# The first whole score tile of a step ahead of the halved tile's first half, and the hold between the two halves on TensorE itself

## The chip, the cores and the metric

The kernel runs on 1 core of one Trainium2 chip. The metric is the device time of one execution in microseconds (us), median of the runs shown.

## What is computed

One transformer-like block on 2048 tokens of width 512, all in float32. With `xn` the layer-normed input:

```python
xn = _layernorm(x, axis=-1)
s = _A_ref(xn, A_wqkv, A_wo)                            # attention, 32 heads of width 16
g = _silu(_B_ref(xn, B_w1, B_b1, B_w2, B_b2))           # gelu MLP, 512 -> 1376 -> 512
return x + s * g
```

The attention is the plain one: scores `q k^T / 4`, softmax over the 2048 keys, times `v`, heads concatenated, times `wo`.

## The kernel before

**Precision and stages.** Operands are split into a high and a low part and multiplied in three terms. A first stage (up to about 480 us of the span) does the layer norm, the projections and the MLP, and already a part of the score tiles described below. The second stage, on which the change bears, is the attention proper: 512 steps and a last one (`for n in range(L + 1)`, line 967). The last 20 steps also do the output projection.

**Units and steps.** The work is cut into 32 units, `u` = one group of 4 heads by one chunk of 512 queries. Each unit takes 16 steps, one for each block of 128 keys. A step does, for its unit and key block:

- **T**, four times (`t_one`, line 733): a transposed score matmul, 128 keys by 512 queries, into a bank of PSUM (L740), and its exponential on ScalarE into SBUF (L742). The row maximum of the scores stands in the matmul as two more rows of the contraction (50 rows = 48 + 2), so it must be known before.
- **V** (`pv_step`, line 799): the four heads' value matmuls of the step before (L805), 32 columns each.

**The score tiles for the maximum.** The maxima come from a second pass over the same scores, 128 queries by 512 keys, that runs ahead: a matmul (`s_mm`, L183) and a maximum on VectorE (`s_max`, L189), in two halves of 256 keys. A job is two such tiles, for head `a` = 0 and `a` = 1 of a pair. Head 0 uses contraction rows from 0 up, head 1 rows from 64 up, so that two matmuls can run side by side in the array; T0 and T1 use the rows from 64 up, T2 and T3 those from 0 up.

A step of the main kind (`want` = 3, steps 2 to 491) does three score tiles. Its order on every engine's queue is a string, written out by hand: `ORDER[3]`, line 40, read by the loop at line 971 and `s_op` (line 209):

- `T`, `V`: as above.
- `S`: a whole tile of 512 keys (`s_whole`, line 198). The first S of a step takes a new job from `jobs` and does head 0, the second does its head 1.
- `X` and `Y`: a cut tile, 256 keys of both heads of another job, in one bank. X (lines 217 to 224) does head 0 into the left half of the bank. Y (lines 226 to 233) does head 1 into the right half, then one maximum over both. The other 256 keys come with the X and Y of the next step.

X and Y write one bank from different rows of the array, so Y must not start before X is done. In the kernel before, a `nop` on GpSimd waits for X (lines 221 and 222), and Y waits for that `nop` (line 228).

**The banks.** The score tiles take turns in three PSUM banks, `s_ring` (line 90; a third one is added at line 774). S takes the first bank of the ring and puts it at the end; X takes one and holds it until Y, which puts it back (line 230). A tile's matmul waits for VectorE's maximum of the tile that had the bank before. T has four banks, one of them used by every fourth T, so T waits for ScalarE's exponential of the T four before.

**Bookkeeping that rides along.** When the last maximum of a unit is issued, `s_end0` (line 239) queues a small maximum on VectorE, puts off two small operations on GpSimd (lines 251 and 252) to the next X (`run_off`, line 224) and has SyncE load the queries of the unit after next. Each V counts four ticks; eight ticks later (`later`, `flush`) a transpose on TensorE (L268) and a copy send the maxima to DRAM. At the end of a unit ScalarE copies the value sums out of PSUM (L812). The schedule is fixed when the program is built; the engines wait for each other by semaphores only.

Of the kernel before, what the change touches and what calls it, by code (L numbers as in the profile page):

```python
# [36 lines left out]
FILL0 = 30  # L37
HB = 4
W2B = 2
ORDER = {0: "TTTTV", 3: "TXSTTSTYV"}  # L40
HC = CH // 2
PAIRED = 28
KB = 3
# [5 lines left out]
def fused(ctx: ExitStack, tc: tile.TileContext, x, wqk, wv, wo, w1, b1, w2, b2, out):  # L49
    nc = tc.nc  # L50
# [35 lines left out]
    SYNC = mybir.DependencyInfo(mybir.DependencyClass.Sync, mybir.DependencyReason.DATA)  # L86
# [5 lines left out]
    def s_tile(held=False):  # L92
        pool = s_ring.pop(0)
        if not held:
            s_ring.append(pool)
        return pool.tile([P, CH], F32, name="ps"), pool
# [58 lines left out]
    done = {u: 0 for u in range(NU)}  # L155
# [16 lines left out]
    def at_of(job):  # L172
        u, st, p = job
        return divmod(st, NCH) if u % (NCH * KB) else divmod(st, NCH)[::-1]

    def s_mm(ps, job, a, c0, k0, w):
        u, st, p = job
        qi, ki = at_of(job)
        if u not in MX:
            MX[u] = qring.tile([P, GH, NCH, NCH, 2], F32, name="mx")  # L180
        r = slice(64 * a, 64 * a + 3 * DH)
        k0 += ki * CH
        return nc.tensor.matmul(ps[:, c0:c0 + w], QS[u][r, p, qi * P:(qi + 1) * P],  # L183
                                kts[u // NCH % KB][p][r, k0:k0 + w], start=True, stop=True).ins

    def s_max(ps, job, heads, parts):
        u, p = job[0], job[2]
        qi, ki = at_of(job)
        nc.vector.tensor_reduce(MX[u][:, 2 * p:2 * p + 2, qi, ki][:, heads, parts], ps.rearrange("p (n c) -> p n c", c=HC), axis=AX.X, op=OP.max)  # L189
        done[u] += 1  # L190
        if ended:
            s_end0(ended.pop())
        if done[u] == 64:
            ended.append(u)
        if done[NU - 1] == 64:
            s_end0(ended.pop())

    def s_whole(job, a):
        ps = s_tile()[0]
        s_mm(ps, job, a, 0, 0, CH)  # L200
        s_max(ps, job, a, slice(0, 2))
# [5 lines left out]
    jobs, whole, cut, put_off = [], [], [], []  # L207

    def s_op(op):
        if op == "S":  # L210
            if whole:
                s_whole(whole.pop(), 1)
            else:
                whole.append(jobs.pop(0))
                s_whole(whole[0], 0)
        elif op == "X":
            if not cut:
                cut[:] = [jobs.pop(0), 0]
            ps, pool = s_tile(True)
            x = s_mm(ps, cut[0], 0, 0, cut[1] * HC, HC)  # L220
            token = nc.gpsimd.nop().ins
            tc.add_manual_dep(token, x.name, SYNC, reason="row tile done")
            cut[2:] = [ps, pool, token]
            run_off()
        else:
            job, n, ps, pool, token = cut
            y = s_mm(ps, job, 1, HC, n * HC, HC)
            tc.add_manual_dep(y, token.name, SYNC, reason="other row tile")
            s_max(ps, job, slice(0, 2), n)
            s_ring.append(pool)  # L230
            cut[1] += 1
            if n:
                cut.clear()

    def run_off():
        while put_off:
            put_off.pop(0)()
# [76 lines left out]
    for j in range(len(pairs)):  # L314
        for h in range(2):
# [9 lines left out]
            n = 2 if nd < len(parts) and parts[nd][2] and ready - nd > room else 1  # L325
            n = max(n, need - 2 * (left - 1))
# [233 lines left out]
    s_when, put, row = [], [0], [0, 0]  # L560
# [387 lines left out]
    for t in range(NW):  # L948
        n = DONE + 2 * t
# [6 lines left out]
    for i, t in enumerate(late):  # L956
        n = L - 2 * len(late) - 1 + 2 * i
# [9 lines left out]
    for n in range(L + 1):  # L967
        ua, ka = divmod(n, 16)
        want = due(n) - due(n - 1)
        i = 0  # L970
        for op in ORDER[want] if n > 1 else ("TTTTV", "TTSTSVT")[n]:
            if op in "SXY":
                s_op(op)
            elif op == "V":
                if n:
                    pv_step(*divmod(n - 1, 16))
                for _ in range(4):
                    tick()
                flush()
            else:  # L980
                if EARLY <= 4 * n + i < 4 * L:
                    t_one(ua, ka, i % 2, 1 - i // 2)
                for f, args in todo.get((n, i), []):
                    f(*args)
                i += 1
# [54 lines left out]
```

## Time and profile before

| | us |
|---|---|
| median of 3 runs | 1596.07 (1595.79 to 1596.75) |
| span of the profiled execution | 1594.7 |
| TensorE matmuls busy | 1587.6 (100%) |
| TensorE weight loads busy | 913.2 (57%) |
| VectorE busy | 1382.8 (87%) |
| ScalarE busy | 1260.1 (79%) |
| GpSimd busy | 373.0 (23%) |

The span is the time of the profiled execution from its first to its last instruction; what lies around it belongs to the run. PE is TensorE's matmuls, PEld its weight loads (each matmul's load has a row of its own), DVE VectorE, ACT ScalarE, POOL GpSimd, SP SyncE; a q behind the name is the engine's sequencer. A row of the timeline has the start in us from the span's start, the time that the row covers, the engine, line, operation, tiles (out<-in) and how many instructions are merged in it; in brackets stands the idle time of the engine before it and who ended it. Matmuls are pipelined: their starts overlap the ones before, and a busy PE is not yet a PE at its peak.

### The profile page before, as it was taken

The page shows a single profiled execution, that of the slowest core. Times are in us where ns is not written, and L with a number is a line of the kernel's source. Part 1 is how long each engine was busy: PE and PEld are TensorE (multiplying, and loading weights), DVE is VectorE, ACT ScalarE, POOL GpSimd, SP SyncE. Part 2 cuts the span into 40 slices and gives each one's busy share as a digit, 9 for nine tenths or more (in the row PEclk, how much of TensorE's full clock was granted, in tenths as well). Part 3 has the DMA queues.
Part 4 walks back from the last instruction along what each step waited for, and adds up shares of the span by engine and source line. Part 5 has one row for each costly group of instructions (what it writes and reads, how often), then busy time and mean ns, then how long its engine had stood idle before and what let it go on. Part 6 is the DMA issues. An engine that isn't in the chain of part 4 may idle for free.

```text
span 1594.7 us, 32234 instructions
## 1 busy us (share of the span) xinstructions
PE 1587.6 (100%) x12144; PEld 913.2 (57%) x12144; DVE 1382.8 (87%) x2261; ACT 1260.1 (79%) x2520; POOL 373.0 (23%) x394
## 2 busy tenths in 40 slices
PE   9999999999999999999999999999999999999998
PEld 8899999999884444444444444444444444444445
DVE  7598898989888999999999989999999999999735
ACT  4324333434349999999999999999999999999984
POOL 4145575756650001000100200100010000000142
PEclk9999999999999999999999999999999999999999
DMA  6626343454431113111410411311131111110252
GB/s 205 150 59 164 106 135 107 158 140 123 126 93 54 32 35 66 29 39 44 82 30 21 71 40 30 61 39 29 31 70 30 31 29 36 36 29 22 59 192 100
DMA packets 74651, 116.89 MB, mean 73 GB/s; under 512 B 23012, under 2 KB 24292, under 8 KB 73320
## 3 DMA queue, kind: packets, MB, share of 16 engines
q1 hardware_dynamic: 70748, 101.89, 22.8%
q0 software_dynamic: 3264, 12.35, 3.9%
q8 instruction: 96, 1.57, 0.4%
q14 instruction: 59, 0.48, 0.1%
q10 hardware_dynamic: 484, 0.60, 0.1%
HBM read 84.35 MB, written 25.97 MB: 69 GB/s over the span
## 4 chain that ended last, share of the span: by engine, by line
PE 98%; DVE 1%; DMA 1%; POOL 0%; issue 0%; ACT 0%; SPq 0%; DVEq 0%; POOLq 0%
PE pv L805 32%; PE ps L183 18%; PE pst L740 16%; PE ps L591 12%; PE pst L591 7%; PE ps L740 5%; PE ps L80 3%; PE pv L591 2%; PE ps L459 1%; PE pst L80 1%; DMA raw<-in_wqk 0%; DVE st L418 0%; PE pst L441 0%; DMA xt<-in_x 0%; PE pst L459 0%
## 5 line engine op out<-in xcount | busy, mean ns | idle before, releaser
L189 DVE TENSOR_REDUCE mx<-ps 128x2 f32<-128x512 f32 x2048 | 1299.5, 685 | 149.4 <-PE ps L183 68.8
L742 ACT ACTIVATE slot<-pst 128x512 f32<-128x512 f32 x1533 | 831.0, 612 | 21.6 <-PE pst L740 12.7
L805 PE MATMUL pv<-slot,vsb 128*32 128x512 f32 x4096 | 545.3, 605 | 0.0
L183 PE MATMUL ps<-kt,slot 48*128 48x512 f32 (+1 forms) x1364 | 393.5, 376 | 0.0
L740 PE MATMUL pst<-qt,kt 50*128 50x512 f32 x1149 | 372.7, 432 | 0.6 <-DVE gt L673 0.4
L740 PEld LDWEIGHTS pst<-qt,kt 50*128 50x128 f32 x1149 | 178.6, 184 | 279.9 <-ACT slot L742 264.3
L742 ACT ACTIVATE slot<-ps 128x512 f32<-128x512 f32 x515 | 315.5, 613 | 3.7 <-PE ps L740 0.5
L183 PEld LDWEIGHTS ps<-kt,slot 48*128 48x128 f32 x1364 | 210.6, 184 | 34.8 <-DVE mx L189 21.6
L591 PE MATMUL ps<-slot,w1h 64*128 64x512 f32 x1088 | 218.0, 393 | 0.2 <-ACT junk L605 0.2
L183 PE MATMUL ps<-kt,qz 48*128 48x512 f32 x512 | 212.4, 415 | 0.0
L183 PE MATMUL ps<-slot,slot 48*128 48x512 f32 (+1 forms) x598 | 172.8, 376 | 0.0
L740 PE MATMUL ps<-qt,kt 50*128 50x512 f32 x387 | 160.3, 416 | 0.0
L591 PEld LDWEIGHTS ps<-slot,w1h 64*128 64x128 f32 x1088 | 151.4, 185 | 8.3 <-ACT junk L605 2.7
L805 PEld LDWEIGHTS pv<-slot,vsb 128*32 128x32 f32 x4096 | 80.6, 108 | 120.2 <-issue 112.2
L591 PE MATMUL ps<-slot,w1l 64*128 64x512 f32 x544 | 141.7, 393 | 0.0
L378 POOL TENSOR_TENSOR hl<-hg,hh 128x512 fp32r<-128x512 f32 x76 | 96.7, 1295 | 129.6 <-ACT hh L377 82.5
L605 ACT ACTIVATE junk<-ident_r 1x1 f32<-1x1 f32 x92 | 18.0, 196 | 120.8 <-PE pst L591 113.6
L740 PE MATMUL pst<-qt,slot 50*128 50x512 f32 x384 | 112.5, 415 | 0.0
L251 POOL CAST nmh<-nm 128x16 fp32r<-128x16 f32 x32 | 6.3, 197 | 413.7 <-PE pst L740 184.7
L183 PEld LDWEIGHTS ps<-kt,qz 48*128 48x128 f32 x512 | 93.7, 183 | 16.3
L183 PEld LDWEIGHTS ps<-slot,slot 48*128 48x128 f32 x598 | 92.5, 184 | 15.7 <-DVE mx L189 10.9
L740 PEld LDWEIGHTS ps<-qt,kt 50*128 50x128 f32 x387 | 71.1, 184 | 44.0 <-ACT slot L742 42.8
(159 smaller groups left out, 1699.7 us busy)
## 6 DMA issues: line engine op xcount, KB each, us to landing
raw<-in_w SPq DMA_DIRECT2D x88, 256.0 KB
qk_h<-hh SPq DMA_DIRECT2D x32, 256.0 KB
qk_l<-hl SPq DMA_DIRECT2D x32, 256.0 KB
qt<-qk_h SPq DMA_DIRECT2D x128, 64.0 KB
slot<-qk_h SPq DMA_DIRECT2D x92, 64.0 KB
g_d<-gt POOLq DMA_DIRECT2D x16, 256.0 KB, 3.5
qt<-qk_l SPq DMA_DIRECT2D x64, 64.0 KB
dn<-den_d SPq DMA_DIRECT2D x32, 128.0 KB
```

What stands on the lines that cost most here:

```text
L80: nc.tensor.matmul(ps, lhs[a], rhs[b], start=first and n == 0, stop=last and n == 2)
L183: return nc.tensor.matmul(ps[:, c0:c0 + w], QS[u][r, p, qi * P:(qi + 1) * P], kts[u // NCH % KB][p][r, k0:k0 + w], start=True, stop=True).ins
L189: nc.vector.tensor_reduce(MX[u][:, 2 * p:2 * p + 2, qi, ki][:, heads, parts], ps.rearrange("p (n c) -> p n c", c=HC), axis=AX.X, op=OP.max)
L251: nc.gpsimd.tensor_copy(hl[:, 0], nm)
L378: nc.gpsimd.tensor_sub(hl, raw, hh.bitcast(F32))
L459: nc.tensor.matmul(pq["q", g, c], W1[g][i][:, k * P:(k + 1) * P], (xh, xl)[j][c][:, k], start=n == 0 and k == 0, stop=n == 2 and k == KT - 1)
L591: i = nc.tensor.matmul(ps, lhs[r], rhs[r], start=first, stop=last).ins
L605: i = nc.scalar.activation(junk[:, :1], ident_r[:1, :1].bitcast(F32), AF.Copy).ins
L740: nc.tensor.matmul(ps, kts[g % KB][p][r, k * P:(k + 1) * P], QT[u][r, p, :], start=True, stop=True)
L742: nc.scalar.activation(PT[u, k][:, 2 * p + a, :], ps, AF.Exp, scale=SCALE)
L805: nc.tensor.matmul(PV[u][32 * j:32 * j + 32, :], vsb[:, k, h:h + 32], PT[u, k][:, j, :], start=(k == 0), stop=(k == NT - 1))
```

## The change

The first S of a step moves to the head of the step, before T0 and X. The wait of Y for X is made by TensorE: a `nop` on TensorE ahead of Y waits for X's own semaphore, and the `nop` on GpSimd goes. As the program is built, this wait stands at Y's matmul.

```diff
-ORDER = {0: "TTTTV", 3: "TXSTTSTYV"}
+ORDER = {0: "TTTTV", 3: "STXTTSTYV"}
...
             x = s_mm(ps, cut[0], 0, 0, cut[1] * HC, HC)
-            token = nc.gpsimd.nop().ins
-            tc.add_manual_dep(token, x.name, SYNC, reason="row tile done")
-            cut[2:] = [ps, pool, token]
+            cut[2:] = [ps, pool, x]
             run_off()
         else:
-            job, n, ps, pool, token = cut
-            y = s_mm(ps, job, 1, HC, n * HC, HC)
-            tc.add_manual_dep(y, token.name, SYNC, reason="other row tile")
+            job, n, ps, pool, x = cut
+            hold = nc.tensor.nop().ins
+            tc.add_manual_dep(hold, x.name, SYNC, reason="row tile done")
+            s_mm(ps, job, 1, HC, n * HC, HC)
             s_max(ps, job, slice(0, 2), n)
             s_ring.append(pool)
```

Since the ring of banks turns with the order, X now takes the bank of the second whole tile of the step before, and the first whole tile takes again the bank that it had.

## The prediction, made before the changed kernel ran

> **What bounds the kernel now.** I read the page first, then the busy times of the long second stretch, then who waited for whom in it, and last the order of time of a few of its steps.
>
> ```profile
> span 1594.7 us, 32234 instructions
> ...
> PEclk9999999999999999999999999999999999999999
> ```
>
> The profiled execution spans 1594.7 us, the median of the runs shown is 1596.07, so 1.4 us lie around the span. The clock is full everywhere.
>
> ```profile
> 481.00:1506.00 1025.00, 1025.00 (x7837) 438.64 (x7829) 933.68 (x1532) 1009.78 (x1987) 75.17 (x124) 1.00 0.18 40
> ```
>
> ```profile
> L221 POOLq EVENT_SEMAPHORE  x490: 17/17/17, 479.6 to 1505.8; - x164
> ```
>
> The columns of the first row are the sum and then PE, PEld, DVE, ACT, POOL. The second row is the token that the change removes: one per step of the kind "three score tiles", so 490 steps lie in those 1025 us, 2.09 us each. PE seems full and ACT nearly so (1010 of 1025), which would leave nothing to gain. The waits say otherwise:
>
> ```profile
> PEld pst L740 <- ACT slot L742: 303.0, 396, 0.8
> ...
> DVE mx L189 <- PE ps L183: 63.4, 252, 0.5
> ...
> PEld ps L183 <- DVE mx L189: 32.6, 188, 0.3
> ...
> PEld ps L183 <- POOLq L221: 0.4, 1, 0.4
> ```
>
> VectorE waits for score matmuls and score matmuls wait for VectorE: a loop. The 303 us in the first row are mostly not a wait: the next rows show that the 0.84 us gap of the weight loader is the time in which the four value matmuls (V) stream. GpSimd's token costs 0.4 us in one step and nothing else.
>
> Now two steps in order of time: weight loads, then matmuls, VectorE, ScalarE.
>
> ```profile
> 902.76 0.18 PEld L740 LDWEIGHTS pst<-qt,kt 50*128 50x128 f32 x1 [0.84 <-ACT slot L742]
> 902.76 0.18 PEld L183 LDWEIGHTS ps<-kt,slot 48*128 48x128 f32 x1
> ...
> 902.87 0.19 PEld L183 LDWEIGHTS ps<-kt,slot 48*128 48x128 f32 x1
> ...
> 903.30 0.18 PEld L183 LDWEIGHTS ps<-kt,slot 48*128 48x128 f32 x1
> ...
> 903.85 0.16 PEld L805 LDWEIGHTS pv<-slot,vsb 128*32 128x32 f32 x8 [0.25 <-issue]
> 904.85 0.18 PEld L740 LDWEIGHTS pst<-qt,kt 50*128 50x128 f32 x1 [0.84 <-ACT slot L742]
> ...
> 905.41 0.18 PEld L740 LDWEIGHTS ps<-qt,kt 50*128 50x128 f32 x1
> ...
> 905.90 0.16 PEld L805 LDWEIGHTS pv<-slot,vsb 128*32 128x32 f32 x8 [0.23 <-issue]
> 906.90 0.18 PEld L740 LDWEIGHTS pst<-qt,kt 50*128 50x128 f32 x1 [0.84 <-ACT slot L742]
> ...
> 907.45 0.18 PEld L183 LDWEIGHTS ps<-kt,slot 48*128 48x128 f32 x1
> ```
>
> ```profile
> 902.76 0.50 PE L740 MATMUL pst<-qt,kt 50*128 50x512 f32 x1
> 902.77 0.61 PE L183 MATMUL ps<-kt,slot 48*128 48x256 f32 x2
> ...
> 903.33 0.48 PE L183 MATMUL ps<-kt,slot 48*128 48x512 f32 x1
> 903.45 0.39 PE L740 MATMUL ps<-qt,kt 50*128 50x512 f32 x1
> 903.65 0.28 PE L183 MATMUL ps<-kt,slot 48*128 48x256 f32 x1
> ```
>
> ```profile
> 901.97 1.28 DVE L189 TENSOR_REDUCE mx<-ps 128x2 f32<-128x512 f32 x2
> 903.42 1.89 DVE L189 TENSOR_REDUCE mx<-ps 128x2 f32<-128x512 f32 x3 [0.17 <-PE ps L183]
> 905.50 1.89 DVE L189 TENSOR_REDUCE mx<-ps 128x2 f32<-128x512 f32 x3 [0.20 <-PE ps L183]
> ```
>
> ```profile
> 903.30 1.57 ACT L742 ACTIVATE slot<-pst 128x512 f32<-128x512 f32 x3
> 904.75 0.62 ACT L742 ACTIVATE slot<-ps 128x512 f32<-128x512 f32 x1
> 905.39 1.57 ACT L742 ACTIVATE slot<-pst 128x512 f32<-128x512 f32 x3
> ```
>
> Call the step's four transposed-score matmuls T0 to T3, its whole score tiles S1 and S2, the halves of the cut tile X and Y. A step is T0 X S1 T1 T2 S2 T3 Y V, and T1 and T0, S2 and Y use rows 64 up, the others rows 0 up, two at a time. VectorE takes S1, S2, Y in that order. From 902.76 to 906.90 two steps take 4.14 us, and one closed loop fills them: S2's weights load at 903.30, 0.05 after VectorE's last maximum of the step before (901.97 + 1.28), whose bank it takes. Y follows at 903.65, V at 903.85, the next T0 at 904.85, then X, then S1, whose maximum begins at 905.50; three maxima, 1.89, end at 907.39, and S2 loads at 907.45. That is 903.30 to 907.45, 4.15: **the VectorE loop is the bound**, once round in two steps.
>
> **What the change does to it.** S1 takes T0's place at the head of the step. X and S1 share rows 0 up, so now S1 starts where X started. The pair X, S1 ends at 902.77 + 0.61 = 903.38; a 512-wide matmul that starts the step ends at 902.76 + 0.50 = 903.26. S1 reaches VectorE 0.12 sooner, and the loop falls from 4.14 to 4.02 per two steps. T0 stays beside it, as X stood beside T0 (two weight loads at 902.76), on the other rows; I take its end as unmoved. X moves behind S1 in the same rows; a 256-wide matmul ends 0.12 behind the 512-wide one ahead of it (903.33 + 0.48 = 903.81, then 903.65 + 0.28 = 903.93), so X ends at 0.50 + 0.12 = +0.62 of the step's start. Nobody reads X before Y is done, and T1, T2, S2, T3 keep their places. The banks turn differently: X now takes the bank of S2's maximum of the step before, S1 its own of the step before. Three maxima take 1.89 and two 1.28, so S2's ends 0.61 ahead of Y's, at 902.64; X's weights will be wanted where S1's now load, second in those rows, at 902.87. That wait is free, by 0.2. Since S1 now draws its tile before X does, a unit's last maximum, and with it the 16-wide maximum on VectorE, the two small GpSimd operations (issued at X, as now) and SyncE's loads of the queries two units on, move by less than a step; what needs them comes eight ticks, two steps, later at the earliest. I cost that at nothing.
>
> Next in line are two loops. TensorE alone, from a step where neither engine holds it:
>
> ```profile
> 757.19 0.16 PEld L805 LDWEIGHTS pv<-slot,vsb 128*32 128x32 f32 x8 [0.25 <-issue]
> 758.19 0.18 PEld L740 LDWEIGHTS pst<-qt,slot 50*128 50x128 f32 x1 [0.84 <-ACT slot L742]
> ...
> 758.82 0.18 PEld L183 LDWEIGHTS ps<-kt,slot 48*128 48x128 f32 x1
> 759.21 0.16 PEld L805 LDWEIGHTS pv<-slot,vsb 128*32 128x32 f32 x8 [0.20 <-issue]
> ```
>
> ```profile
> 758.19 0.49 PE L740 MATMUL pst<-qt,slot 50*128 50x512 f32 x1
> ```
>
> V to V is 2.02, 4.04 for two. ScalarE: T0's weights load at 902.76, its exponential starts at 903.30 (0.54); the four of them end at 904.75 + 0.62 = 905.37 (2.07); T3 of the next step takes that buffer and loads at 905.41 (0.04). From there to V there is a price only where T3 is the last thing V waits for, behind the output copy of a unit:
>
> ```profile
> 781.85 0.18 PEld L740 LDWEIGHTS pst<-qt,slot 50*128 50x128 f32 x1 [0.21 <-ACT slot L742]
> ...
> 782.27 0.16 PEld L805 LDWEIGHTS pv<-slot,vsb 128*32 128x32 f32 x8 [0.23 <-issue]
> ```
>
> ```profile
> 780.17 0.65 ACT L742 ACTIVATE slot<-ps 128x512 f32<-128x512 f32 x1
> 780.65 1.65 ACT L742 ACTIVATE slot<-pst 128x512 f32<-128x512 f32 x3
> 782.08 0.70 ACT L742 ACTIVATE slot<-ps 128x512 f32<-128x512 f32 x1
> 782.56 1.85 ACT L742 ACTIVATE slot<-pst 128x512 f32<-128x512 f32 x3
> ```
>
> 0.42, and V to T0 is 1.00. Sum 0.54 + 2.07 + 0.04 + 0.42 + 1.00 = **4.07 for two steps**: the ScalarE loop is the next bound, ahead of TensorE's 4.04 and VectorE's 4.02. So of 0.12 only 0.07 is got. That ScalarE isn't itself full is in the last rows: back to back, exponentials start 0.48 apart (780.17, 780.65, and four later 782.08), 1.92 per step.
>
> **The hold.** The token on GpSimd goes (490 of 17 ns, off the path); TensorE's own wait stands, in the built program's order, at Y itself: no instruction is added. Behind a late Y only V queues, and behind V the next step. Y's weights take 0.11 (a 512-wide matmul with its load exposed takes 0.50, at 902.76, with it hidden 0.39, at 903.45), and Y starts 0.20 before V (903.65 to 903.85); V at the new pace stands at 2.035 - 1.00 = +1.04, so Y may load as late as +0.73, 0.11 behind X's end. The trace has no wait of TensorE on itself that is tight. From below: one hop, a matmul's end to ScalarE or VectorE, is 0.04 (903.26 to 903.30, 903.38 to 903.42), ScalarE's to TensorE 0.04. From above: the old way by GpSimd, two hops, T0's end 758.19 + 0.49 = 758.68 to Y's load at 758.82, 0.14. I take 0.05, the nearest row being one hop into TensorE (903.25 to 903.30); at that the hold costs nothing; at 0.14 the step is 1.00 + 0.62 + 0.14 + 0.31 = 2.07, all the gain gone.
>
> **The sum.** 490 steps are 245 pairs. At each of about 30 unit ends the output copy enters ScalarE's queue; the 0.21 wait at 781.85 shows that such a pair goes by ScalarE already, so it gains nothing, and it takes back what the pair ahead of it won, since ScalarE's queue is where it was. 245 - 60 = 185 pairs x 0.07 = 13 us. The code ahead of 480 us and the tail behind 1506 are unchanged. 1594.7 - 13 + 1.4 = **1583 us**. The terms are rounded to 0.01 each, so the gain is 9 to 17 by itself: 1579 to 1587.
>
> **The rivals.**
> - *ScalarE's hold isn't felt* (T3's lateness hides behind Y) and TensorE's own 4.04 decides: 185 x 0.10 and some of the pairs at unit ends, 20 us, 1576. Against: 781.85.
> - *ScalarE sets the pace already*, as its 1010 of 1025 says: nothing to win, 1594 to 1598. Against: the 0.48 spacing, and VectorE's wait of 0.17 to 0.20 in every step, which would not end with S1.
> - *The hold opens a little late*, between 0.11 and 0.14 behind X's end: Y sets V. At 0.12 the step is 1.00 + 0.62 + 0.12 + 0.31 = 2.05, two are 4.10, 185 x 0.04 = 7 us, 1589. Against: T0's end frees ScalarE 0.04 later although X ends beside it. The Trainium skill, "TensorE: Matmul & The Clock Gate", section "The cost: per-tile semaphore tail", speaks for it: completion increments of concurrent tiles queue up, 25 + 4.7 per tile + 26.3 per increment in ns, an estimate of 0.12 for S1, T0 and X together. By that rule this would be the result; the 0.04 of the rows shows no such tail so far.
> - *The change doesn't do what it says*: T0 comes late behind S1, as weight loads go one by one. Every ns lands in the ScalarE loop; from 0.07 the gain is gone, at a whole load, 0.11, two steps take 4.18, +7 us, 1603. Against: the two loads at 902.76.
> - *Slower: the hold opens late.* TensorE's wait on its own end, ahead of Y in every step, takes more than 0.14 and sets V. Each 0.01 beyond costs 490 x 0.01 = 5 us; at 0.20, 1.00 + 0.62 + 0.20 + 0.31 = 2.13, 490 x 0.06, about 1625; if it opens only when T3 has ended too, 0.4 and more per step, 200 us. For: no row shows such a wait. Against: single hops are 0.04 to 0.05.
>
> **Chances.** Forecast (1579 to 1587) 0.48, TensorE's pace 0.12, no change 0.14, hold a little late 0.08, T0 late 0.07, hold late 0.11. The range goes down to TensorE's pace with the rounding, 1573, and up to the late T0, 1603; it leaves out the late hold and little else. A measurement of this kernel tells 0.2%, 3.2 us, from no change. Faster 0.48 + 0.12 + 0.08 = 0.68, same 0.14, slower 0.07 + 0.11 = 0.18.
>
> **What would show it.** In the changed profile: the first 512-wide L183 matmul with the step's first weight load; VectorE's maxima starting 0.12 sooner after it; L183's waits for VectorE near nothing; T3's loads waiting for ScalarE in ordinary steps; V to V at 2.03 to 2.04. Wrong if Y's load stands more than 0.73 behind the step's first load, or if T0's exponential starts later than 0.54 behind it.

## The result and the profile after

The changed kernel takes 1590.08 us (median of 5, 1589.65 to 1590.31) against 1596.01 of the kernel before in the same session: ratio 0.9962, 95% interval 0.9951 to 0.9973, 5.9 us less. The forecast was 13 us less: the right way, and the time lies inside the range, but the gain is less than half of what was forecast.

The page and the waits of the changed kernel between 481 and 1501 us (total, times, longest). Line numbers behind the edit are one lower than before.

```profile
span 1588.3 us, 31761 instructions
```

```profile
PEld ps L183 <- DVE mx L189: 399.0, 476, 0.8
...
DVE mx L189 <- PE pst L739: 34.9, 150, 0.5
...
DVE mx L189 <- PE ps L183: 17.0, 76, 0.5
...
PEld pst L739 <- ACT slot L741: 12.9, 54, 0.8
...
DVE mx L189 <- PE ps L739: 11.3, 48, 0.5
```

The first row looks like a new wait of 399 us and isn't one: it is the 0.84 us in which V streams, now put down to S1, since S1's load is the first behind V. VectorE's idle time ahead of a maximum is 34.9 + 17.0 + 11.3 = 63.2 here, where it was 63.4: no less, although S1 comes sooner. That sum alone names no bound, since VectorE waited as long in the kernel before, where its loop set the pace; the rows in order of time and the experiments have to.

Two steps of the changed kernel in order of time, weight loads, then two matmuls, then VectorE and ScalarE:

```profile
899.90 0.18 PEld L183 LDWEIGHTS ps<-kt,slot 48*128 48x128 f32 x1 [0.84 <-DVE mx L189]
899.91 0.18 PEld L739 LDWEIGHTS pst<-qt,kt 50*128 50x128 f32 x1
...
900.58 0.18 PEld L739 LDWEIGHTS ps<-qt,kt 50*128 50x128 f32 x1
...
901.01 0.16 PEld L804 LDWEIGHTS pv<-slot,vsb 128*32 128x32 f32 x8 [0.24 <-issue]
902.01 0.18 PEld L183 LDWEIGHTS ps<-kt,slot 48*128 48x128 f32 x1 [0.84 <-DVE mx L189]
902.01 0.18 PEld L739 LDWEIGHTS pst<-qt,kt 50*128 50x128 f32 x1
...
902.59 0.18 PEld L739 LDWEIGHTS ps<-qt,kt 50*128 50x128 f32 x1
902.68 0.18 PEld L183 LDWEIGHTS ps<-kt,slot 48*128 48x128 f32 x1
903.03 0.16 PEld L804 LDWEIGHTS pv<-slot,vsb 128*32 128x32 f32 x8 [0.16 <-issue]
```

```profile
902.01 0.50 PE L183 MATMUL ps<-kt,slot 48*128 48x512 f32 x1
...
902.35 0.27 PE L183 MATMUL ps<-kt,slot 48*128 48x256 f32 x1
```

```profile
902.55 1.29 DVE L189 TENSOR_REDUCE mx<-ps 128x2 f32<-128x512 f32 x2 [0.22 <-PE ps L183]
```

```profile
900.48 1.57 ACT L741 ACTIVATE slot<-pst 128x512 f32<-128x512 f32 x3
901.92 0.62 ACT L741 ACTIVATE slot<-ps 128x512 f32<-128x512 f32 x1
902.58 1.08 ACT L741 ACTIVATE slot<-pst 128x512 f32<-128x512 f32 x2
```

Read them against the same rows of before. S1's maximum begins 902.55 - 902.01 = 0.54 behind the step's first load, where it was 903.42 - 902.76 = 0.66: the 0.12 are there. T0's exponential begins 902.58 - 902.01 = 0.57 behind T0's load (900.48 - 899.91 = 0.57 in the step before), where it was 0.54: **T0 frees ScalarE 0.03 later**. T3's load at 900.58 stands 0.05 behind the end of the exponential that held its buffer, and V follows 0.43 later. The ScalarE loop, T0's load to exponential, four exponentials, T3's load, V, next T0, is now 0.57 + 2.06 + 0.05 + 0.43 + 1.00 = 4.11 for two steps instead of 4.07 (2.06 is 902.54 - 900.48, from the start of T0's exponential to the end of T3's), against 4.14 of the VectorE loop before: 0.03 to 0.04 are won per pair, not 0.07. The 185 pairs of the forecast times 0.03 give 5.6 us; 5.9 were measured. The hold isn't in it: X ends at 902.35 + 0.27 = 902.62, Y's load follows at 902.68, 0.67 behind the step's first load. V stands at 903.03 - 902.01 = 1.02 in this step; with the 0.31 that the prediction puts between Y and V, Y could wait until 0.71.

### The profile page after: what moved, and what is told of

The parts are those of the page before. It is cut to its first block, busy times and chain, and to the rows that moved or that the text cites. A ratio compares the mean times of both kernels' runs of the same rounds, so it can differ in the third digit from the quotient of the medians.

```text
span 1588.3 us, 31761 instructions
## 1 busy us (share of the span) xinstructions
PE 1581.8 (100%) x12144; PEld 934.7 (59%) x12144; DVE 1379.1 (87%) x2261; ACT 1259.1 (79%) x2520; POOL 373.7 (24%) x394
## 4 chain that ended last, share of the span: by engine, by line
PE 97%; ACT 1%; DVE 1%; issue 0%; DMA 0%; ACTq 0%; DVEq 0%
PE pv L804 33%; PE ps L183 24%; PE ps L590 12%; PE pst L739 10%; PE pst L590 7%; PE ps L739 3%; PE ps L80 3%; PE pv L590 2%; PE ps L458 1%; ACT slot L741 1%; PE pst L80 1%; DVE st L417 0%; PE pst L440 0%; DMA xt<-in_x 0%; PE pst L458 0%
## 5 line engine op out<-in xcount | busy, mean ns | idle before, releaser
L183 PEld LDWEIGHTS ps<-kt,slot 48*128 48x128 f32 x1364 | 223.8, 184 | 280.2 <-DVE mx L189 278.3
L183 PE MATMUL ps<-kt,slot 48*128 48x512 f32 x1364 | 379.4, 365 | 0.0
L739 PEld LDWEIGHTS pst<-qt,kt 50*128 50x128 f32 x1149 | 188.6, 184 | 41.8 <-ACT slot L865 12.6
L183 PEld LDWEIGHTS ps<-slot,slot 48*128 48x128 f32 x598 | 98.3, 184 | 121.5 <-DVE mx L189 120.7
L183 PE MATMUL ps<-slot,slot 48*128 48x512 f32 x598 | 166.0, 364 | 0.0
L842 POOL TENSOR_TENSOR ot<-ot,dn 64x512 f32<-64x512 f32 x15 | 19.6, 1304 | 299.7 <-DMA dn<-den_d 256.9
```

The costliest lines, as they stand in the source:

```text
L739: nc.tensor.matmul(ps, kts[g % KB][p][r, k * P:(k + 1) * P], QT[u][r, p, :], start=True, stop=True)
L842: eng.tensor_mul(ot[c][rs, g // 2], ot[c][rs, g // 2], DN.pop(u)[rs])
```

## The experiments

Theory: the order makes the gain, the hold is nearly nothing, and half of the gain is lost because S1 and T0 end together and TensorE tells of their ends one after the other, S1 first. Rivals: TensorE's wait on itself eats it; X behind S1 eats it; VectorE still bounds.

**1. T0 first again, S1 second.**

```diff
-ORDER = {0: "TTTTV", 3: "STXTTSTYV"}
+ORDER = {0: "TTTTV", 3: "TSXTTSTYV"}
```

> The changed kernel with T0 back at the head and S1 second: order T S X T T S T Y V, TensorE's own hold kept. Theory: the gain lost in the changed kernel is T0's release. S1 and T0 end together, TensorE tells of their ends one after the other, about 0.03 us apart in program order, and T0, being second, frees ScalarE 0.03 late in a loop that sets the pace. With T0 first that goes to S1, whose VectorE loop has that much room: two steps take 4.07 instead of 4.10, T0's exponential starts 0.54 behind its weight load again, S1's maximum 0.03 later behind S1's; the time is 6 us below the changed kernel, about 1584. Rival 1 (TensorE's wait on itself is what eats the gain): the hold is the same, the time stays at 1590. Rival 2 (X behind S1 is what costs): X is still behind S1, 1590.

Measured 1583.03 us against 1596.41 of the kernel before, ratio 0.9917 (0.9903 to 0.9931): 13.4 us less than before. Its weight loads, ScalarE and VectorE:

```profile
897.11 0.18 PEld L739 LDWEIGHTS pst<-qt,kt 50*128 50x128 f32 x1 [0.84 <-ACT slot L741]
...
897.74 0.18 PEld L739 LDWEIGHTS ps<-qt,kt 50*128 50x128 f32 x1
...
898.16 0.16 PEld L804 LDWEIGHTS pv<-slot,vsb 128*32 128x32 f32 x8 [0.19 <-issue]
899.16 0.18 PEld L739 LDWEIGHTS pst<-qt,kt 50*128 50x128 f32 x1 [0.84 <-ACT slot L741]
...
899.76 0.18 PEld L739 LDWEIGHTS ps<-qt,kt 50*128 50x128 f32 x1
```

```profile
897.64 1.57 ACT L741 ACTIVATE slot<-pst 128x512 f32<-128x512 f32 x3
899.09 0.62 ACT L741 ACTIVATE slot<-ps 128x512 f32<-128x512 f32 x1
899.70 1.57 ACT L741 ACTIVATE slot<-pst 128x512 f32<-128x512 f32 x3
```

```profile
899.73 1.29 DVE L189 TENSOR_REDUCE mx<-ps 128x2 f32<-128x512 f32 x2 [0.17 <-PE ps L183]
```

The 0.03 have changed places: T0's exponential is back at 0.54 (899.70 - 899.16), S1's maximum has gone from 0.54 to 0.57. The ScalarE loop is 0.53 + 2.07 + 0.05 + 0.42 + 1.00 = 4.07. Hold and X are as in the changed kernel, so the rivals that blame them fall. This version beats both kernels.

The trace of this run also answers another rival, that VectorE is late because ScalarE begins to read its own tile at the same moment. Behind the output copy of a unit ScalarE is busy when T0 ends and takes it later. Weight loads, ScalarE and VectorE of such a step:

```profile
611.23 0.18 PEld L739 LDWEIGHTS pst<-qt,kt 50*128 50x128 f32 x1 [0.84 <-ACT slot L741]
611.24 0.18 PEld L183 LDWEIGHTS ps<-kt,slot 48*128 48x128 f32 x1
```

```profile
611.95 1.67 ACT L741 ACTIVATE slot<-pst 128x512 f32<-128x512 f32 x3
```

```profile
611.81 0.69 DVE L189 TENSOR_REDUCE mx<-ps 128x2 f32<-128x512 f32 x1 [0.21 <-PE pst L739]
```

T0's exponential begins only at 611.95, and S1's maximum still begins 611.81 - 611.24 = 0.57 behind S1's load. All 60 such steps of the stretch are like this.

**2. The new order alone, with the old token on GpSimd.**

```diff
-ORDER = {0: "TTTTV", 3: "TXSTTSTYV"}
+ORDER = {0: "TTTTV", 3: "STXTTSTYV"}
```

> The new order alone, S T X T T S T Y V, with the old token on GpSimd between X and Y. Theory: the gain comes from the order; the longer way over GpSimd brings Y's weight load to +0.72 to +0.76 of the step, still about where Y is wanted, so the time is 1590 to 1592, 4 to 6 us below the kernel before. Rival 1 (the wait of TensorE on itself costs): faster than the changed kernel, 1584 to 1587. Rival 3 (the gain is the lifted token, not the order): back at 1596.

Measured 1590.91 us against 1596.41, ratio 0.9967 (0.9954 to 0.9979). The order alone brings 5.5 us, where both together bring 5.9; the intervals don't tell the two apart. Two weight loads of a step, S1's and Y's, and X's matmul:

```profile
900.19 0.18 PEld L183 LDWEIGHTS ps<-kt,slot 48*128 48x128 f32 x1 [0.84 <-DVE mx L189]
...
900.91 0.18 PEld L183 LDWEIGHTS ps<-kt,slot 48*128 48x128 f32 x1
```

```profile
900.53 0.28 PE L183 MATMUL ps<-kt,slot 48*128 48x256 f32 x1
```

Y loads 0.72 behind the step's first load, as expected, and 0.10 behind X's end (900.53 + 0.28 = 900.81). The prediction's 0.14 for the way over GpSimd was counted from T0's end, though the token waits for X.

**3. The hold alone, in the old order.**

```diff
-ORDER = {0: "TTTTV", 3: "STXTTSTYV"}
+ORDER = {0: "TTTTV", 3: "TXSTTSTYV"}
```

(on the changed kernel, so that TensorE's own wait stays)

> The old order T X S T T S T Y V with TensorE's own hold in place of GpSimd's token. Theory: 1595 to 1596, since the VectorE loop of 4.14 per two steps has no part of Y's wait in it; only the few steps with a late token can win, 1 us. Rival 1 (TensorE's wait on itself costs time): above 1597. Rival 3 (the gain is the lifted token): 1590.

Measured 1596.29 us against 1596.41, ratio 0.9999 (0.9990 to 1.0008): no difference.

**4. The hold made later: Y waits for T1 too.** T1 is the next matmul behind X.

```diff
             cut[2:] = [ps, pool, x]
+            since_x.clear()
...
             tc.add_manual_dep(hold, x.name, SYNC, reason="row tile done")
+            tc.add_manual_dep(hold, since_x[0], SYNC, reason="next of the tiles too")
```

(each T puts its matmul's name into `since_x`)

> The changed kernel with Y held behind T1 as well, the next matmul after X, which ends about 0.12 us after it. It measures what a later hold costs. Theory: one hop into TensorE is 0.05, so Y loads at about +0.78 of the step, V follows 0.31 later, a step takes 2.09 to 2.10 with no alternation left, and the time is 10 to 15 us above the kernel before, 1606 to 1611. Rival 1 (the wait opens much later than one hop, and was binding already in the changed kernel): the full 0.12 per step on top of the changed kernel, 490 x 0.12 = 57 us, about 1647. If the hold has more room than I think: 1590 to 1596.

Measured 1607.02 us against 1596.41, ratio 1.0067 (1.0054 to 1.0081), 10.6 us more. T0 and T1 in one row, and two loads:

```profile
907.16 0.73 PE L742 MATMUL pst<-qt,kt 50*128 50x512 f32 x2
```

```profile
906.16 0.16 PEld L807 LDWEIGHTS pv<-slot,vsb 128*32 128x32 f32 x8
...
907.95 0.18 PEld L183 LDWEIGHTS ps<-kt,slot 48*128 48x128 f32 x1
908.26 0.16 PEld L807 LDWEIGHTS pv<-slot,vsb 128*32 128x32 f32 x8
```

T1 ends at 907.16 + 0.73 = 907.89 and Y loads at 907.95: TensorE's wait on itself takes 0.06, here where it sets V's place as in the changed kernel, where it doesn't (902.62 to 902.68). V follows 0.31 later and the step is 2.10, as the sum in the prediction has it (1.00 + 0.79 + 0.31).

**5 and 6. Less work for VectorE, in the kernel before and in the changed one.**

```diff
-        nc.vector.tensor_reduce(MX[u][:, 2 * p:2 * p + 2, qi, ki][:, heads, parts], ps.rearrange("p (n c) -> p n c", c=HC), axis=AX.X, op=OP.max)
+        src = ps.rearrange("p (n c) -> p n c", c=HC)
+        if "seen" not in prog and heads in (0, 1):
+            src = src[:, :, :HC // 2]
+        nc.vector.tensor_reduce(MX[u][:, 2 * p:2 * p + 2, qi, ki][:, heads, parts], src, axis=AX.X, op=OP.max)
...
-        nc.scalar.activation(PT[u, k][:, 2 * p + a, :], ps, AF.Exp, scale=SCALE)
+        nc.scalar.activation(PT[u, k][:, 2 * p + a, :], ps, AF.Exp, scale=SCALE / 8)
```

> The kernel before with less work for VectorE: in the attention stage the maximum of a whole score tile reads only half of each 256 keys (the maxima are then not the row's, and the exponential's scale is cut to an eighth so that nothing overflows; no instruction is added or removed). It opens the VectorE loop and leaves everything else. Theory: what bounds then is the ScalarE loop of 4.07 per two steps, since T0 still stands first and frees ScalarE 0.54 behind its load: 12 to 15 us below the kernel before, 1581 to 1584, although ScalarE, TensorE and the order are untouched. Rival (the kernel before is bound by ScalarE's or TensorE's own time): 1594 to 1596.

> The changed kernel with the same cut in VectorE's maxima (same part left out). Theory: nothing to win, 1588 to 1590, because the changed kernel goes by the ScalarE loop with T0's release 0.03 late, 4.10 per two steps; so it is slower than the kernel before with the same cut, by 5 to 7 us. Rival (the changed kernel is still bound by VectorE, and its maxima start late): 1581 to 1584, level with the other.

In the kernel before: 1582.05 us against 1596.36, ratio 0.9909 (0.9896 to 0.9923). In the changed one: 1589.94 us, ratio 0.9958 (0.9946 to 0.9971), the same as with the whole maxima. In the kernel before, T0's load, its exponential and VectorE's maxima are now:

```profile
902.74 0.18 PEld L743 LDWEIGHTS pst<-qt,kt 50*128 50x128 f32 x1 [0.84 <-ACT slot L745]
```

```profile
903.27 1.57 ACT L745 ACTIVATE slot<-pst 128x512 f32<-128x512 f32 x3
```

```profile
903.41 1.36 DVE L192 TENSOR_REDUCE mx<-ps 128x2 f32<-128x256 f32 x3 [0.68 <-PE ps L183]
```

The three maxima take 1.36 instead of 1.89, VectorE waits 0.68 for the next, and T0 still frees ScalarE 0.53 behind its load. So VectorE's loop bounds the kernel before and no longer bounds the changed one; and with VectorE out of the way the old order is the faster by 7.9 us (5 to 7 were expected). These two runs differ in the order and in the hold; that it is T0's place that counts is shown by the pairs that differ in it alone: experiment 1 and the changed kernel, and experiments 7 and 2.

**7. Order of the first experiment with the old token.** Edit: the kernel before with `3: "TSXTTSTYV"`.

> Order T S X T T S T Y V with the old token on GpSimd in place of TensorE's own hold. Theory: Y's load comes at +0.72 to +0.76, still free at a step of 2.035 but with less room; 1583.5 to 1585.5, so the hold is worth 0.5 to 2 us. If the hold is what makes this order pay: 1588 and more.

Measured 1584.29 us against 1596.36, ratio 0.9924 (0.9911 to 0.9938). Against experiment 2, which has the same token and only S1 and T0 the other way round, T0 first is worth 6.6 us. The hold would be worth 1.3 us in this order (12.1 against 13.4 us below the kernel before), but the two intervals overlap.

**8. X first, T0 second.** Edit: the kernel before with `3: "XTSTTSTYV"`.

> Order X T S T T S T Y V with the old token: X ahead of T0, else as the kernel before. X ends 0.1 ahead of T0, so T0's end is told next to X's. Theory: S1 still comes after X, so the VectorE loop of 4.14 is unchanged; whatever T0's release loses, up to 0.03, lies in a loop that has 0.07 of room: 1595 to 1597. If a late T0 costs by itself, whatever the bound: 6 us more than the kernel before, 1602.

Measured 1595.86 us against 1596.36, ratio 0.9996 (0.9987 to 1.0005): no difference. Its first two matmuls of a step, T0's load and the exponential:

```profile
904.11 0.39 PE L183 MATMUL ps<-kt,slot 48*128 48x256 f32 x1
904.11 0.49 PE L740 MATMUL pst<-qt,kt 50*128 50x512 f32 x1
```

```profile
904.11 0.18 PEld L740 LDWEIGHTS pst<-qt,kt 50*128 50x128 f32 x1
```

```profile
904.64 1.57 ACT L742 ACTIVATE slot<-pst 128x512 f32<-128x512 f32 x3
```

T0's load is the second of the step, as in the changed kernel, and its exponential begins 0.53 behind it, not 0.57. Standing second, or loading second, costs nothing here; in the runs it cost when the matmul ahead in the program ended at the same time. X, 256 wide, ends 0.1 earlier (0.39 against 0.49); S1, 512 wide, ends with T0. I had left open whether T0 would be late here: it isn't.

**All steps together.** The rows above are single steps, and 0.03 is near the last digit. These are the medians over all steps between 481 and 1488 us, worked out from the traces of the runs, in us: T0's load to its exponential, the step's first load to S1's maximum, and V to the second next V.

| order, hold or maxima | T0 to ScalarE | S1 to VectorE | two steps |
|---|---|---|---|
| kernel before, `TXSTTSTYV` | 0.54 | 0.66 | 4.14 |
| changed, `STXTTSTYV` | 0.57 | 0.54 | 4.11 |
| 1, `TSXTTSTYV` | 0.54 | 0.57 | 4.08 |
| 2, `STXTTSTYV`, token | 0.57 | 0.54 | 4.11 |
| 3, `TXSTTSTYV`, TensorE's hold | 0.54 | 0.66 | 4.14 |
| 4, `STXTTSTYV`, Y behind T1 | 0.57 | 0.54 | 4.20 |
| 5, kernel before, short maxima | 0.54 | 0.66 | 4.08 |
| 6, changed, short maxima | 0.57 | 0.54 | 4.11 |
| 7, `TSXTTSTYV`, token | 0.54 | 0.57 | 4.08 |
| 8, `XTSTTSTYV`, token | 0.54 | 0.65 | 4.14 |

## Why the prediction was right and wrong

- **The bound of the kernel before, the VectorE loop of 4.14**: right; experiment 5 opens it and gains what the next bound allows.
- **S1's place and its 0.12**: right to the hundredth (0.66 to 0.54).
- **The ScalarE loop as the next bound, at 4.07**: right as a place. Experiments 1 and 5 land on it (13.4 and 14.3 us, forecast of its price 13). The count of pairs fits as well: laid unit for unit beside the kernel before, the median unit of 16 steps is 0.40 shorter in experiment 1 and 0.18 in the changed kernel, and six of its eight pairs at the differences of the unrounded medians of two steps (4.141 to 4.076 and to 4.113) would give 0.39 and 0.17. In experiment 1 every fourth unit is 0.48 to 0.60 shorter, which the count doesn't have and nothing here explains.
- **The step that failed: "T0 stays beside it ... I take its end as unmoved."** The recorded end is unmoved (0.50 behind its start, as in experiment 2's trace of the same order; a matmul's end in the profile is modelled), but ScalarE starts 0.03 later, and the ScalarE loop is 4.11, not 4.07. The gain per pair is 0.03 instead of 0.07: a term put at nothing took half of the gain. The ground given, that X had stood beside T0 in the same way, doesn't hold: X ends before T0, S1 ends with it. The prediction named the sign itself, an exponential later than 0.54 behind T0's load; it stands at 0.57.
- **The rival "T0 comes late behind S1"** had the right place and the right rule, that every ns lands in the ScalarE loop, and two wrong things: its cause was the weight load, which experiment 8 excludes (in the changed kernel, too, T0's load stands at 902.01 with S1's), and its chance was 0.07.
- **The rival "the hold opens a little late"** had 1589, next to the measured 1590, by luck: Y's wait took 0.06 where it needed 0.12, and experiment 1 keeps the hold and takes 1583.
- **The rule set aside.** The Trainium skill, "TensorE: Matmul & The Clock Gate", section "The cost: per-tile semaphore tail", gives 26.3 ns for each completion increment that queues. The prediction applied it to the hold, where it didn't matter, and found no tail in the rows, since T0 frees ScalarE 0.04 behind its end "although X ends beside it". That reading was wrong. T0 is the first of the two in the program, and in the kernel before X ends at 904.85 + 0.38 = 905.23, T0 at 904.85 + 0.50 = 905.35, 0.12 later:

```profile
904.85 0.50 PE L740 MATMUL pst<-qt,kt 50*128 50x512 f32 x1
904.85 0.38 PE L183 MATMUL ps<-kt,slot 48*128 48x256 f32 x1
```

So this pair couldn't show a tail. For the second of two matmuls that do end together the size agrees with the rule: 0.03 between 0.54 and 0.57, for T0 in the changed kernel and for S1 in experiment 1.

- **The hold**: right. 0.06 for TensorE's wait on itself (0.05 taken), free in this order; against the token it is worth 1.3 us at most, which the intervals don't tell from nothing (experiments 2, 3, 7). What a late Y costs came out as reckoned in experiment 4.

That the 0.03 is a queue of announcements, and not two ends that are truly 0.03 apart, is not settled: the runs show only that it falls on the second in program order of two matmuls whose recorded ends are together, on neither when the one ahead ends 0.1 earlier, and that it doesn't need the other reader to start at that moment (experiment 1).

## What to carry to other kernels

When a loop between engines is the bound, write down the next loops with all their terms before a change: the gain ends at the second one, and a few hundredths of a us in it are as large as the gain. Of two matmuls side by side that end together, put first the one whose reader is in the tighter loop. An idle time or a busy share doesn't name the bound: in the kernel before ScalarE is busy 1010 of 1025 us and VectorE 934, yet VectorE's loop set the pace, and less work for VectorE alone made the kernel 14.3 us faster (experiment 5).

## What the runs showed of the hardware that I had not expected

The reader of the second of two matmuls that end together starts 0.03 us later than the reader of the first (0.57 against 0.54), whichever of ScalarE and VectorE it is, and for VectorE also where ScalarE is still busy with something else. A TensorE wait for its own earlier matmul opens 0.06 us behind that matmul's recorded end, hardly more than T3's wait for ScalarE (0.05); by way of a `nop` on GpSimd it opens 0.10 behind (experiment 2).
